# The first four units of a linear-attention kernel with a bilinear FFN: other places for loads, transfers and engine work

## The chip, the cores and the metric

The kernel runs on one core of one Trainium2 chip. The metric is the device time of one execution in microseconds (us), as a median of several runs. Before the change it is 614.28 us (three runs, 614.20 to 614.68).

## The reference

For each of 4 batches and 8 heads of width 48 a state of 48x48 is carried over 768 tokens; its result goes through a bilinear FFN.

```python
f = 1.0 / (1.0 + np.exp(-f_logit))
for t in range(S):                       # B, H, S, D = 4, 8, 768, 48
    state = f[:, :, t, :, None] * state + np.einsum('bhd,bhe->bhde', k[:, :, t], v[:, :, t])
    y[:, :, t] = np.einsum('bhd,bhde->bhe', q[:, :, t], state)
x = y.transpose(0, 2, 1, 3).reshape(B * S, H * D)         # 3072 x 384
out = (x @ w_a) * (x @ w_b) @ w_out                        # 384 -> 1536 -> 384
```

The inputs q, k, v and f_logit are float32. The three weights arrive as 64-bit floats, and the kernel makes float32 of them on the chip.

## The kernel before

**Units and blocks.** A unit is four heads of one batch over 384 tokens (BLK). Two units with the same tokens give the 384 columns of x for one block, so units 0 and 1 belong to block 0, units 2 and 3 to block 1, and there are 16 units and 8 blocks. What the change touches is the stretch in which units 0 to 3 run while the weights are still arriving; from unit 4 on a planner (`by_quotients`, from L1072) lays the work of the units beside the FFN's matmuls, with costs and due times that are written in the code.

**One unit** has these steps, each a function with one engine or two:
- `load_unit` (L196) issues its DMAs on the queue of SyncE (SP): two each for f, k and q, one for v. Three sets of buffers are used in turn, so unit 3 uses the set of unit 0.
- `front_parts` (L291) has four parts. Part 0 is two sigmoids on ScalarE (ACT) and a multiply-add on GpSimd (POOL). Parts 1 and 2 are running products on VectorE (DVE, L311 and L324). Part 3 multiplies k and q by them (L328). `next(fronts[u])` issues the next part.
- On TensorE (PE): `scores` (L382), `turn` (L406, a transposition of k), `within` (L480), `gains` (L430) and `across` (L501). Between them `mask` (L395, DVE), `turned` (L413 and L415, ACT) and `carried`/`carry` (L458 and L460, DVE, six small additions that carry the state from chunk to chunk). `hand_on` (L469) scales the last state for the next 384 tokens.
- `out_of_bank` (L520) copies y out of PSUM in three parts, on ACT or DVE. `stored` issues the transfers of y into xT (`store`, L542): five DMAs from SBUF to SBUF for each unit, since 48 rows of a head don't fall on whole blocks of 128.

**The FFN's first product.** `up(blk, ft)` (matmuls at L586) makes 128 of the 1536 columns of x @ w_b and x @ w_a for one block: 3 slices of x for b, then 3 for a, and each float32 matmul shows as two records, so 12 records for one `up`. It needs all of the block's xT. `product` copies b out of PSUM (ACT, L606) and multiplies (DVE, L608). Four PSUM banks serve two `up`s.

**The weights.** `weight_pieces` cuts them into 14 pieces of w_b and w_a, in turns (pieces 0 and 1 hold the columns of ft 0, 2 and 3 those of ft 1 and 2, 4 and 5 of ft 3 and 4, 6 and 7 of ft 5 and 6, and so on), and 6 of w_out. `load_weights` (L249, SP) loads the next piece into one of four places, or for pieces 4 and 5 into `groups`. `from_double` converts a piece: ACT L58 and L59 and POOL L60, then ACT L62 and L63, then DVE L68 and L70, which writes the float32 weights. `begin(n)` issues the steps of ACT and POOL up to piece n (begin(7.5) only the first half of the eighth), `end(n)` the DVE step up to n pieces; `end` also loads a further piece when it has ended one from the third on.

**What sets the order.** Each engine works in the order in which the code from L949 to L1069 issues the steps: the change touches this order, written out by hand. The queue of SP is in order too. The DMAs use eight semaphores in turn, so that a DMA is issued only when the one eight places ahead of it has landed. The buffers `at`, `kT` and `y` exist once; PSUM tiles ps_x and ps_y hold scores, transposed k, gains and y of a unit: for unit 2 its y is in ps_x, which unit 3's `turn` writes.

After the first five `up`s of block 0 a loop over `ups` converts a piece and runs an `up` in each turn, alternating blocks.

Of the kernel before, what the change touches and what calls it, by code (L numbers as in the profile page):

```python
# [48 lines left out]
        yield to, rows.rearrange("(k p) c -> p k c", p=128), (2, DM)  # L49


def from_double(nc, dst, raw, k, h, bit, sgn, whole):

    words = raw.bitcast(U32).rearrange("p k (n two) -> p (k n) two", two=2)
    lo, hi = words[:, :, 0], words[:, :, 1]
    width = lo.shape[1]
    h, bit, sgn = (x[:, 0:width] for x in (h, bit, sgn))
    nc.scalar.activation(h, hi.bitcast(FP32), AF.Abs, scale=HI_SCALE)  # L58
    nc.scalar.activation(bit.bitcast(FP32), lo, AF.Identity, bias=whole, scale=2.0**-29)  # L59
    nc.gpsimd.tensor_scalar(h, h, HI_MAX, None, ALU.min)  # L60
    yield
    nc.scalar.activation(sgn, hi.bitcast(FP32), AF.Sign)  # L62
    nc.scalar.activation(  # L63
        bit.bitcast(U16).rearrange("p (n two) -> p n two", two=2)[:, :, 1], sgn, AF.Relu, scale=-32768.0
    )
    yield
    hu = h.bitcast(U32)
    nc.vector.tensor_scalar(hu, hu, 3, None, ALU.logical_shift_left)  # L68
    hu, bit = (x.rearrange("p (k n) -> p k n", k=k) for x in (hu, bit))
    nc.vector.tensor_tensor(dst.bitcast(U32), hu, bit, ALU.add)  # L70
    yield


# [60 lines left out]
def by_quotients(ctx, tc, q, k, f_logit, v, moe_w_a, moe_w_b, moe_w_out, out, ident, weights, bad):  # L134
    nc = tc.nc
# [60 lines left out]
    def load_unit(u, names="fkqv"):  # L196
        for do in loads_of(u, names):
            do()
# [37 lines left out]
    def load_weights(n=1):  # L236
        for _ in range(n):
            if len(raws) == len(todo):
                return
            dst, src, (k, m) = todo[len(raws)]  # L240
            raw = dst
            if src.dtype != FP32:

                if len(raws) in EARLY:
                    raw = groups[:, EARLY.index(len(raws))].bitcast(mybir.dt.uint64)
                else:
                    raw = next(raw_places)
                raw = raw[:, 0:k * m].rearrange("p (k m) -> p k m", k=k)
            nc.sync.dma_start(out=raw, in_=src)  # L249
            raws.append(raw)  # L250

    def begin(n):

        while 2 * n > begun[0] < 2 * len(todo):
            i, second = divmod(begun[0], 2)
            dst, src, shape = todo[i]
            if not second:
                going.append(
                    from_double(nc, dst, raws[i], shape[0], next(blocks), bits[i % len(bits)], sign, whole)
                    if src.dtype != FP32 else iter(())  # L260
                )
            next(going[i], None)
            begun[0] += 1
# [153 lines left out]
    def gains(u, chunks=range(NC)):  # L417

        _, half, _ = unit(u)
        t, kT = sets[u % NSET], live[u]["kT"]  # L420
        last = half == NH - 1
        ps = live[u]["turned"]
        for n in range(2):
            for c in chunks:
                for p in range(2):
                    if last and c == NC - 1 and p == 1:
                        continue
                    for h in range(2):
                        r = slice(SUB * p, SUB * p + SUB)
                        nc.tensor.matmul(  # L430
                            ps[p][R * h:R * h + D, (n * NC + c) * D:(n * NC + c) * D + D],
                            lhsT=kT[r, n, c, R * h:R * h + D],
                            rhs=t["v"][r, n, c, h * D:h * D + D],
                            start=True,
                            stop=True,
                        )
        if chunks[0]:
            return
        st = sb3.tile([128, NJ, 2, D], FP32, tag="st", name="st")
        before = live[u - NQ]["st"][NJ] if half else None  # L440
        live[u]["st"] = [before] + [st[:, j] for j in range(NJ - 1 if last else NJ)]

    def carried(u, js=range(NJ)):

        for j in js:
            if j + 1 < len(live[u]["st"]):
                carry(u, j)
        if js[-1] == NJ - 1:
            hand_on(u)
            give_back(live[u]["turned"])  # L450

    def carry(u, j):
# [9 lines left out]
    def hand_on(u):  # L462

        if unit(u)[1] == NH - 1:
            return
        before = live[u]["st"][-1]
        for n in range(2):
            end = products_of_f[u][:, n, BLK - 1:BLK]
            nc.vector.tensor_scalar(before[:, n], before[:, n], end, math.exp(-MIDDLE), ALU.mult, ALU.mult)  # L469
# [40 lines left out]
    def out_of_bank(u, part):  # L510

        if not part:
            if u == NQ - 1:

                live[u]["y_sb"] = groups[:, 2 * NTG - 1, PIECE:].rearrange("r (o p m) -> r o p m", p=2, m=SUB)
            else:
                live[u]["y_sb"] = sb1.tile([128, 2 * NC, 2, SUB], FP32, tag="y", name="y")
        p, e, r, rows = ((0, 0, 0, 128), (1, R, 0, D), (1, 0, R, D))[part]
        copy = nc.vector.tensor_copy if u in FIRST and p else nc.scalar.copy
        copy(live[u]["y_sb"][r:r + rows, :, p], live[u]["y"][p][e:e + rows, 0:BLK].rearrange("r (o m) -> r o m", m=SUB))  # L520

    def stored(u):
# [6 lines left out]
    def stores_of(u):  # L529

        b, half, qd = unit(u)
        blk = b * NH + half

        def begin():
            if qd == 0:
                xT[blk] = sb2.tile([128, NKT, BLK], FP32, tag="xT", name="xT")
            live.pop(u - NQ, None)

        def store(n, h, kt, p, row, w):
            y = live[u]["y_sb"].rearrange("r (n c) p m -> r n (c p m)", n=2)  # L540
            queue = nc.scalar if u == NQ - 1 and n else nc.sync
            queue.dma_start(out=xT[blk][p:p + w, kt], in_=y[row:row + w, n])  # L542

        yield begin
        for n in range(2):
            for h in range(2):
                ch, row, left = (4 * qd + 2 * n + h) * D, R * h, D
                while left:
                    kt, p = divmod(ch, 128)
                    w = min(left, 128 - p)  # L550
                    yield partial(store, n, h, kt, p, row, w)
                    ch, row, left = ch + w, row + w, left - w
# [21 lines left out]
    def up(blk, ft):  # L574

        for _, _, _, do, *args in up_steps(blk, ft):
            do(*args)
# [353 lines left out]
    with tc.manual_schedule():  # L931
# [11 lines left out]
        def y_of(u):  # L943
            for part in range(3):
                out_of_bank(u, part)
            stored(u)
# [7 lines left out]
        for u in FIRST:  # L954
# [2 lines left out]
            load_weights()  # L957
            load_unit(u, "v")
        load_unit(2, "f")
        load_weights()  # L960
        for _ in range(3):
            next(fronts[0])
# [14 lines left out]
        carried(0, range(4))  # L977
        within(0)
        gains(1, range(NC - 1))
        mask(1)  # L980

        carried(1, range(1))
        carried(0, range(4, NJ))
        within(1)
        gains(1, range(NC - 1, NC))
        across(0)
        load_weights()
        carried(1, range(1, NJ))
        y_of(0)
        begin(3)  # L990
        across(1)
        y_of(1)
        end(2)


        load_unit(2, "k")
        load_unit(2, "q")
        load_weights()
        load_unit(2, "v")
        load_unit(3, "f")  # L1000
        load_weights()
        load_unit(3, "k")
        load_unit(3, "q")
        load_unit(3, "v")
        up(0, 0)
        begin(4)
        next(fronts[2])
        end(3)
        next(fronts[2])
        product()  # L1010
        end(4)
        next(fronts[2])
        load_unit(4, "f")
        up(0, 1)
        next(fronts[3])
        turn(2)
        turned(2)
        scores(2)
        mask(2)
        product()  # L1020
        begin(5)
        next(fronts[3])
        up(0, 2)
        within(2)
        gains(2)
        carried(2)
        begin(6)
        product()
        across(2)
        end(5)  # L1030
        y_of(2)
        load_weights()
        end(6)
        next(fronts[3])
        next(fronts[3])
        up(0, 3)
        product()
        begin(7)
        turn(3)
        turned(3)  # L1040
        scores(3)
        mask(3)
        up(0, 4)
        within(3)
        gains(3)
        carried(3)
        product()
        end(7)
        across(3)
        y_of(3)  # L1050
        load_unit(4, "k")
        load_unit(4, "q")
        load_unit(4, "v")
        load_weights()
        begin(8)
        end(8)


        ups = [(1, 0)]
        for i in range(5, NFT):  # L1060
            ups += [(1, i - 4), (0, i)]
        ups += [(1, i) for i in range(NFT - 4, NFT)]
        alone = len(todo) - 6
        for n, (blk, i) in enumerate(ups[0:alone]):
            convert(needed(i))
# [527 lines left out]
```

## Time and profile before

| | |
|---|---|
| median of three runs | 614.28 us |
| the profiled execution | 615.86 us |
| its span, first to last instruction | 614.1 us |
| busy: PE, weight loads, DVE, ACT, POOL | 574.0, 512.5, 411.4, 268.0, 76.2 us |
| PE busy from 200 to 600 us | 398.3 of 400 us |
| DMA moved | 49.42 MB |
| transfer of y into xT, SP, issue to landing | 2.2 us in the median |
| one `up` at the full clock (150 records in 48.54 us) | 3.9 us |

In the lines of the profile a row of ten or forty slices shows tenths of a slice. PEld is TensorE's weight load, which lies beside the matmuls. "A <- B" in a list of waits says that A waited until B was done, with the sum in us, how often, and the longest. SPq and ACTq are queues that issue DMAs. A group's "x5" is the number of its instructions.

### The profile page before, as it was taken

The page shows a single profiled execution, that of the slowest core. Times are in us where ns is not written, and L with a number is a line of the kernel's source. Part 1 is how long each engine was busy: PE and PEld are TensorE (multiplying, and loading weights), DVE is VectorE, ACT ScalarE, POOL GpSimd, SP SyncE. Part 2 cuts the span into 40 slices and gives each one's busy share as a digit, 9 for nine tenths or more (in the row PEclk, how much of TensorE's full clock was granted, in tenths as well). Part 3 has the DMA queues.
Part 4 walks back from the last instruction along what each step waited for, and adds up shares of the span by engine and source line. Part 5 has one row for each costly group of instructions (what it writes and reads, how often), then busy time and mean ns, then how long its engine had stood idle before and what let it go on. Part 6 is the DMA issues. An engine that isn't in the chain of part 4 may idle for free.

```text
span 614.1 us, 13863 instructions
## 1 busy us (share of the span) xinstructions
PE 574.0 (93%) x5778; PEld 512.5 (83%) x5778; DVE 411.4 (67%) x760; ACT 268.0 (44%) x505; POOL 76.2 (12%) x69
## 2 busy tenths in 40 slices
PE   1586889999999999999999999999999999999995
PEld 1444545555899999899989999999999999999995
DVE  6876424559997778885997569765866255836741
ACT  6627478984212345416541354316441244235300
POOL 6323144545300000000000000000000000000000
PEclk9878979999999999999999999999999999999998
DMA  8486698309955134016001440014001100000000
GB/s 216 142 231 175 181 226 260 128 1 166 187 129 139 36 96 96 3 35 166 23 3 33 114 101 2 2 35 109 1 3 46 36 11 1 1 27 0 1 28 31
DMA packets 33336, 49.42 MB, mean 80 GB/s; under 512 B 3952, under 2 KB 25072, under 8 KB 33264
## 3 DMA queue, kind: packets, MB, share of 16 engines
q1 hardware_dynamic: 30144, 42.53, 25.6%
q0 software_dynamic: 2992, 5.77, 5.6%
q8 instruction: 47, 0.77, 0.5%
q14 instruction: 25, 0.20, 0.1%
q10 hardware_dynamic: 128, 0.15, 0.1%
HBM read 33.23 MB, written 4.72 MB: 62 GB/s over the span
## 4 chain that ended last, share of the span: by engine, by line
PE 82%; DVE 8%; issue 3%; DMA 3%; ACT 2%; POOL 1%; SPq 1%; DVEq 0%; ACTq 0%; POOLq 0%
PE ps_f L708 34%; PE ps_f L801 26%; PE ps_f L586 13%; PE ps_y L501 2%; PE ps_y L480 2%; DVE sums L700 1%; PE ps_x L430 1%; DVE inv L324 1%; PE ps_x L382 1%; PE ps_x L406 1%; DMA groups<-in_moe_w_b_dram 1%; DVE groups L700 1%; POOL sums L60 1%; DMA q_in<-in_q_dram 1%; DVE groups L311 1%
## 5 line engine op out<-in xcount | busy, mean ns | idle before, releaser
L586 PE MATMUL ps_f<-xT,w_ba 128*128 128x384 f32 x288 | 105.1, 525 | 12.6 <-DMA xT<-y 7.4
L586 PEld LDWEIGHTS ps_f<-xT,w_ba 128*128 128x128 f32 x288 | 58.0, 205 | 55.6 <-issue 12.2
L1241 ACT COPY sums<-ps_f 128x384 f32<-128x384 f32 x120 | 57.3, 480 | 76.1 <-PE ps_f L708 59.9
L1241 ACT COPY groups<-ps_f 128x384 f32<-128x384 f32 x120 | 57.7, 481 | 62.9 <-PE ps_f L708 39.9
L708 PE MATMUL ps_f<-xT,w_ba 128*128 128x192 f32 x384 | 78.4, 327 | 0.0
L708 PEld LDWEIGHTS ps_f<-xT,w_ba 128*128 128x128 f32 x384 | 64.8, 190 | 0.2
L708 PE MATMUL ps_f<-groups,w_ba 128*128 128x192 f32 x288 | 55.4, 327 | 0.0
L708 PE MATMUL ps_f<-x_sums,raw 128*128 128x192 f32 x288 | 54.0, 331 | 1.2 <-DVE groups L700 0.9
L801 PE MATMUL ps_f<-w_out,sums 128*128 128x192 f32 x288 | 52.2, 329 | 0.0
L801 PE MATMUL ps_f<-w_out,groups 128*128 128x192 f32 x288 | 51.7, 328 | 0.0
L708 PEld LDWEIGHTS ps_f<-x_sums,raw 128*128 128x128 f32 x288 | 46.9, 190 | 4.3 <-DVE groups L700 1.8
L801 PE MATMUL ps_f<-spare,sums 128*128 128x192 f32 x288 | 49.0, 326 | 0.0
L708 PEld LDWEIGHTS ps_f<-groups,w_ba 128*128 128x128 f32 x288 | 47.9, 190 | 0.5 <-ACT groups L1241 0.3
L60 POOL TENSOR_SCALAR sums<-sums 128x768 f32<-128x768 f32 (+1 forms) x20 | 40.9, 2046 | 58.5 <-ACT sums L58 58.4
L801 PEld LDWEIGHTS ps_f<-w_out,sums 128*128 128x128 f32 x288 | 47.1, 190 | 0.9 <-DVE o L836 0.5
L801 PEld LDWEIGHTS ps_f<-w_out,groups 128*128 128x128 f32 x288 | 47.1, 190 | 0.7
L801 PEld LDWEIGHTS ps_f<-spare,sums 128*128 128x128 f32 x288 | 47.1, 190 | 0.1
L307 POOL TENSOR_SCALAR inv<-inv 128x768 f32<-128x768 f32 x14 | 13.0, 925 | 266.1 <-ACT inv L304 266.0
L700 DVE TENSOR_TENSOR sums<-sums,groups 128x768 f32<-128x768 f32 x36 | 34.7, 965 | 14.2 <-ACT groups L1241 13.7
L700 DVE TENSOR_TENSOR sums<-ps_f,sums 128x384 f32<-128x384 f32 x60 | 32.9, 553 | 16.5 <-PE ps_f L708 15.0
L708 PE MATMUL ps_f<-x_sums,w_ba 128*128 128x192 f32 x192 | 39.3, 327 | 0.5 <-DVE sums L700 0.5
L708 PE MATMUL ps_f<-xT,raw 128*128 128x192 f32 x192 | 39.4, 328 | 0.0
(134 smaller groups left out, 852.2 us busy)
## 6 DMA issues: line engine op xcount, KB each, us to landing
raw<-w_ba POOLq DMA_DIRECT2D x11, 512.0 KB, 8.3
k_in<-in_k_dram SPq DMA_DIRECT2D x32, 144.0 KB, 3.4
q_in<-in_q_dram SPq DMA_DIRECT2D x32, 144.0 KB, 4.1
v_in<-in_v_dram SPq DMA_DIRECT2D x16, 288.0 KB, 5.2
raw<-in_moe_w_out_dram SPq DMA_DIRECT2D x6, 768.0 KB, 4.3
out_dram<-o SPq DMA_DIRECT2D x24, 192.0 KB, 2.0
f_in<-in_f_logit_dram SPq DMA_DIRECT2D x28, 144.0 KB, 3.0
xT<-y SPq DMA_DIRECT2D x45, 72.0 KB, 2.2
```

Source lines behind the costliest of these rows:

```text
L60: nc.gpsimd.tensor_scalar(h, h, HI_MAX, None, ALU.min)
L307: nc.gpsimd.tensor_scalar(inv, inv, EXP_K, 1.0, ALU.mult, ALU.add)
L311: nc.vector.tensor_tensor_scan(F[:, c], F[:, c], none, math.exp(MIDDLE), ALU.mult, ALU.add)
L324: nc.vector.tensor_tensor_scan(inv[:, w], inv[:, w], none[:, 0:C], first, ALU.mult, ALU.add)
L382: nc.tensor.matmul(ps[h][SUB * p:SUB * p + SUB, o:o + SUB], lhsT=kf[r, tokens(n, c, p)], rhs=qf[r, tokens(n, c, p)], start=True, stop=True,)
L480: nc.tensor.matmul(ps[p][e:e + D, o:o + SUB], lhsT=t["v"][r, n, c, h * D:h * D + D], rhs=at[r, h, o:o + SUB], start=o == 0, stop=True, ski ...
L501: nc.tensor.matmul(ps[p][e:e + D, o:o + SUB], lhsT=st[j][r, n], rhs=qf[r, tokens(n, c, p)], start=False, stop=True, skip_group_check=True,)
L586: nc.tensor.matmul(ps[nm][:, 0:BLK], lhsT=w[:, kt, ft * 128:ft * 128 + 128], rhs=xT[blk][:, kt], start=kt == 0, stop=kt == NKT - 1,)
L700: nc.vector.tensor_tensor(to, x, y, op)
L708: nc.tensor.matmul(ps[:, g], lhsT=sums_of_w[name][:, g, 128 * j:128 * j + 128], rhs=sums_of_x[blk][name], start=start and g == 0, stop=Tru ...
L801: nc.tensor.matmul(to, lhsT=x[:, i // 2, i % 2], rhs=w[:, NI * (i % 2) + i // 2], start=start and i == 0, stop=i == HFT - 1, skip_group_ch ...
L1241: do(*args)
```

## The change

Five things change, all in the stretch of the first four units, and one in the conversion.

1. **Loads.** Pieces 2 and 3, k, q and v of unit 2, f of unit 3 and piece 4 are issued on SP right behind f of unit 2, ahead of the transfers of y of units 0 and 1. Before they stood behind these. Pieces 5 and on stay behind.
2. **y of units 0 and 1.** Both units' copies out of PSUM come ahead of both units' transfers. Of unit 1 two of three copies are on ACT (before one). Unit 0's first two transfers and unit 1's last two go over ACT's queue (before only unit 1's last two).
3. **State.** The last of the six additions and `hand_on` of units 0 and 1 go behind the transfers. `end(1)` (DVE's step of piece 0) goes ahead of unit 1's `mask`, `end(2)` behind the transfers.
4. **Orders of the engines for units 2 and 3.** Among others: all of unit 2's front directly behind `up(0, 0)`, `turn` and `scores` of unit 2 ahead of `up(0, 1)`, `within` and `gains` of unit 2 ahead of `up(0, 2)`, `turn` and `scores` of unit 3 ahead of `up(0, 3)`, and `end(8)` ahead of unit 3's transfers (before behind them).
5. **The loop's order.** `up(0, 5)` comes first, ahead of `up(1, 0)`.
6. **Conversion.** L70 for pieces of w_b and w_a becomes three instructions, one for each slice of 128 rows, where it was one.

```diff
-def from_double(nc, dst, raw, k, h, bit, sgn, whole):
+def from_double(nc, dst, raw, k, h, bit, sgn, whole, apart=False):
...
-    nc.vector.tensor_tensor(dst.bitcast(U32), hu, bit, ALU.add)
+    dst = dst.bitcast(U32)
+
+    for rows in ([slice(i, i + 1) for i in range(k)] if apart else [slice(0, k)]):
+        nc.vector.tensor_tensor(dst[:, rows], hu[:, rows], bit[:, rows], ALU.add)
...
-                    from_double(nc, dst, raws[i], shape[0], next(blocks), bits[i % len(bits)], sign, whole)
+                    from_double(
+                        nc, dst, raws[i], shape[0], next(blocks), bits[i % len(bits)], sign, whole, shape[0] == NKT
+                    )
...
         if js[-1] == NJ - 1:
-            hand_on(u)
             give_back(live[u]["turned"])
...
-        copy = nc.vector.tensor_copy if u in FIRST and p else nc.scalar.copy
+        copy = nc.vector.tensor_copy if u in FIRST and part > u else nc.scalar.copy
...
-            queue = nc.scalar if u == NQ - 1 and n else nc.sync
+            queue = nc.scalar if u in FIRST and n == u else nc.sync
...
         load_unit(2, "f")
+        load_weights(2)
+        load_unit(2, "k")
+        load_unit(2, "q")
+        load_unit(2, "v")
+        load_unit(3, "f")
         load_weights()
...
         gains(1, range(NC - 1))
+        end(1)
         mask(1)
 
         carried(1, range(1))
-        carried(0, range(4, NJ))
+        carried(0, range(4, 5))
         within(1)
         gains(1, range(NC - 1, NC))
         across(0)
-        load_weights()
-        carried(1, range(1, NJ))
-        y_of(0)
-        begin(3)
-        across(1)
-        y_of(1)
-        end(2)
-
-
-        load_unit(2, "k")
-        load_unit(2, "q")
-        load_weights()
-        load_unit(2, "v")
-        load_unit(3, "f")
-        load_weights()
+        carried(1, range(1, 5))
+        for u in FIRST:
+            if u:
+                across(u)
+            for part in range(3):
+                out_of_bank(u, part)
+        for u in FIRST:
+            stored(u)
+        begin(3)
+        end(2)
+        for u in FIRST:
+            carried(u, range(5, NJ))
+            hand_on(u)
+
+
         load_unit(3, "k")
         load_unit(3, "q")
         load_unit(3, "v")
+        load_weights()
         up(0, 0)
+        for _ in range(3):
+            next(fronts[2])
         begin(4)
-        next(fronts[2])
-        end(3)
-        next(fronts[2])
-        product()
+        next(fronts[3])
         end(4)
-        next(fronts[2])
+        turn(2)
+        scores(2)
         load_unit(4, "f")
         up(0, 1)
-        next(fronts[3])
-        turn(2)
-        turned(2)
-        scores(2)
         mask(2)
         product()
+        turned(2)
         begin(5)
         next(fronts[3])
-        up(0, 2)
+        next(fronts[3])
         within(2)
         gains(2)
+        product()
         carried(2)
         begin(6)
-        product()
+        next(fronts[3])
+        up(0, 2)
         across(2)
-        end(5)
+        end(6)
         y_of(2)
         load_weights()
-        end(6)
-        next(fronts[3])
-        next(fronts[3])
-        up(0, 3)
-        product()
-        begin(7)
         turn(3)
         turned(3)
         scores(3)
+        begin(7)
+        product()
+        up(0, 3)
         mask(3)
-        up(0, 4)
+        begin(7.5)
         within(3)
         gains(3)
+        product()
         carried(3)
-        product()
-        end(7)
+        begin(8)
+        up(0, 4)
+        end(8)
         across(3)
         y_of(3)
         load_unit(4, "k")
         load_unit(4, "q")
         load_unit(4, "v")
         load_weights()
-        begin(8)
-        end(8)
-
-
-        ups = [(1, 0)]
-        for i in range(5, NFT):
-            ups += [(1, i - 4), (0, i)]
-        ups += [(1, i) for i in range(NFT - 4, NFT)]
+        product()
+
+
+        ups = [(0, 5), (1, 0)]
+        for i in range(6, NFT):
+            ups += [(1, i - 5), (0, i)]
+        ups += [(1, i) for i in range(NFT - 5, NFT)]
```

## The prediction

> **What bounds the kernel now.** I read the slices of the span first, to find where TensorE (PE) isn't full.
>
> ```profile
> PE   1586889999999999999999999999999999999995
> ACT  6627478984212345416541354316441244235300
> PEclk9878979999999999999999999999999999999998
> DMA  8486698309955134016001440014001100000000
> ```
>
> A slice is 15.35 us. From the sixth on (80 us) PE is full to the end, so that a us is won only ahead of 80 us, and what is won there arrives at the end as long as the later work waits for PE alone. Next, that stretch by windows: PE, weight loads, DVE, ACT, POOL busy, then granted clock, DMA share.
>
> ```profile
> 27.00:31.30 4.30, 0.29 (x18) 0.14 (x6) 3.92 (x9) 2.08 (x4) 0.00 (x0) 0.80 0.30 76
> 31.30:44.40 13.10, 12.07 (x24) 6.16 (x25) 10.89 (x18) 3.41 (x5) 3.32 (x2) 0.67 0.89 239
> 44.40:54.00 9.60, 8.27 (x203) 5.75 (x201) 5.24 (x10) 8.45 (x12) 4.43 (x3) 1.00 1.02 265
> 54.00:58.10 4.10, 0.01 (x1) 0.04 (x1) 2.14 (x4) 3.19 (x6) 1.01 (x1) 0.85 0.12 38
> 58.10:74.40 16.30, 15.01 (x215) 9.52 (x215) 9.03 (x20) 5.18 (x7) 2.12 (x1) 0.83 0.64 188
> 74.40:80.20 5.80, 2.43 (x4) 0.71 (x5) 1.97 (x3) 5.03 (x7) 2.12 (x1) 0.76 0.24 61
> 80.20:84.20 4.00, 3.99 (x7) 2.18 (x8) 0.51 (x1) 2.33 (x4) 0.98 (x1) 0.50 1.06 223
> ```
>
> PE has three holes (27 to 31.3, 54 to 58.1, 74.4 to 80.2), and behind each a stretch at half the clock, where it looks busy and does half the work. The waits from 31 to 81 us say why:
>
> ```profile
> ACT spare L304 <- DMA f_in<-in_f_logit_dram: 8.4, 1, 8.4
> PE ps_f L586 <- DMA xT<-y: 7.4, 3, 4.0
> PE ps_f L586 <- DVE w_ba L70: 4.4, 2, 4.2
> DVE groups L608 <- ACT x_sums L606: 4.3, 2, 3.0
> DVE w_ba L70 <- PE ps_f L586: 1.3, 1, 1.3
> ```
>
> ACT stands 8.4 us (37.1 to 45.5) until unit 3's f has landed, and all conversions behind it in ACT's order come late. So piece 4 is ready (L70) only at 57.9, and `up(0, 3)` waits 4.2 us. The waits for xT are the first and the third hole. The transfers and loads on SP's queue, in order of time:
>
> ```profile
> 27.71 3.20 SPq L542 DMA_DIRECT2D xT<-y  x5
> 31.01 1.81 SPq L542 DMA_DIRECT2D xT<-groups  x3
> 32.91 1.01 SPq L208 DMA_DIRECT2D k_in<-in_k_dram  x2
> 34.92 0.42 SPq L249 DMA_DIRECT2D groups<-in_moe_w_b_dram  x1
> 35.97 0.89 SPq L208 DMA_DIRECT2D f_in<-in_f_logit_dram  x2
> ```
>
> Eight transfers of y take SP 5 us to issue; the last lands at 34.13. Unit 2's and 3's loads stand behind them, though the DMA engines were idle from 23.3 (landing of piece 3) to 27.7.
>
> **What the Trainium skill says.** "TensorE: Matmul & The Clock Gate", Part 1: after an idle window of some 3.4 us PE runs at half its clock, and returns after a busy window; windows run freely. The trace agrees: the granted clock is 0.5 from 29.60 to 39.84, 56.91 to 63.73 and 77.39 to 84.21, all multiples of 3.41. "DMA: Bandwidth & Descriptors", Queues, rings and completion order: SP and ACT own one ring each on the same DMA engines, a ring is worked off in order, and the engines alternate between rings. The trace agrees: piece 5, behind other loads, lands 12.0 us after its issue, a transfer of y with nothing ahead 2.2 us. "SBUF — State Buffer", Who interferes with whom: a DVE operation with two SBUF inputs and a reading POOL operation exclude each other. L60 took 2.65 us beside DVE's scan and 2.12 alone; I add up to 0.5 us per meeting.
>
> **The change, part by part.**
>
> *Loads ahead.* k, q, v of unit 2, f of 3 and piece 4 are 1920 KB. From the landing of unit 2's k (35.76) to piece 7 (56.62) 4944 KB came, 237 KB per us, so they end 8.1 us after piece 3 (23.33): 31.4. f of unit 3 lands near 28 (before 45.4): ACT's 8.4 us go. The price is that SP's transfers of y, issued from 27, stand in the ring behind piece 4 and land after 31.4.
>
> *y over two queues.* Ahead of unit 1's additions DVE has three instructions less (one of 0.27 us, two of 0.25 to 0.8), and ahead of the copies three more of them, so across(1) starts 0.2 to 0.8 us sooner than 26.42, and all copies are done near 27.7 (before 29.6). SP issues six transfers at 0.6 us from 27.1, ACT four at 0.64 from 27.7. The eighth waits for the one eight places ahead, piece 4. The last lands at about 31.4 + 2 = 33.3 (31.5 to 36): 0.8 us sooner than before, not the 2 us that the issue times alone would give. ACT is held some 3 us by issuing; it isn't late for that, since its next work is needed at 38.
>
> *Rows of L70.* One operation is 0.96 us (1536 elements) or 0.56 (768), so 0.16 + 0.52 ns per element; three of 512 cost 1.1 us where they follow on each other. That is 0.2 us more per piece; at least 0, at most 0.5. It stays beside PE. What goes is DVE's wait for PE (1.3 us here, 9.9 us over all pieces): a slice's columns no longer span those that PE reads.
>
> *PE's line*, with one `up` 3.9 us (150 records in 48.54 us) and 7.7 at half clock (12 x 0.64); turn 0.65, scores 0.75, within 0.8, gains 0.65, across 0.7 from the chain:
> - `up(0, 0)`: first slices from 31.7, all from 33.3, at half clock: to 39.4. Meanwhile DVE does end(2) 1.1, the state 1.5, unit 2's front 6.3, pieces 2 and 3 3.3 (to 40.5), none late.
> - turn, scores to 41; `up(0, 1)` to 44.9; within, gains to 46.4 (mask 42; ACT's turned 41); `up(0, 2)` 50.3; across 51.0. Before, the same work was done at 53.9.
> - turn(3) writes ps_x, from which ACT copies unit 2's y: three copies, 1.46: hole to 52.6. scores to 54.0. Piece 4 is ready at 53.5, piece 5 at 55: ACT has both done by 49, at 3.6 us a piece.
> - `up(0, 3)` to 57.9 (before 65). mask(3) stands on DVE behind product of `up(0, 2)`, whose copy stands on ACT behind turned(3) and piece 6: 52.6 + 0.8 + 0.8 + 3.6 + 0.5 = 58.3, product 58.8, mask 59.75: hole of 1.85.
> - within, gains 61.2; `up(0, 4)` 65.1; across(3) 65.8. Unit 3's xT takes 5.65 us from there as before (74.42 to 80.07), so to 71.5; loads of pieces 9 and 10 ahead of it end at about 69.5 (unit 5's loads start at 55.2, and the same row took 9.1 us from first landing to piece 9, then 2.5 for 10) and cost nothing more.
> - `up(0, 5)` lies under that, to 69.7; two slices of `up(1, 0)` to 71; it goes on at 71.5.
>
> Before, `up(1, 0)` went on at 80.2 without `up(0, 5)`. The lead is 80.2 - (71.5 - 3.9) = 12.6. To it comes the half clock from 80.2 to 84.2 that had cost 2.0. The two new holes (1.6 and 1.85) may drop the clock; a window of 3.4 at half costs 1.7, and at somewhat over even odds I take 1.0. **Sum: 13.6 us.** Cover gone: without `up(0, 5)` under the transfers, 3.9 us come back.
>
> *After it.* The loop has ACT busy 4.0 of 3.92 us per turn, yet it needs piece 9 at its sixth turn, and the pieces stand ready some 6 us early (L70 of piece 9 at 97.6, needed at 104), so nothing new is late. The planner's part starts behind the loop in every engine's own order and moves as a whole; ±1 us.
>
> The profiled execution was 615.86 around a span of 614.1, the median 614.28. So 614.1 - 13.6 = 600.5 of span, 602.3 profiled, and **600.7** as a median.
>
> **The rivals.**
> 1. *y late behind the bulk loads.* If piece 4 lands at 33 and the transfers behind the eighth wait for it too, the last lands at 36.2, 2.9 late; one more cold window 1.7, and ACT held at its queue 1.5 more: 606.8. For it: SP's ring is in order, and the eight semaphores. Against: ACT's ring passes it by.
> 2. *The clock in the holes.* Both holes trip it, for one or two windows each: 3.4 to 6.8 instead of 1.0, so 603 to 606.5; I take 604.5. From 73.97 to 77.39 PE was busy 1.3 us and fell; from 70.56 to 73.97 it was busy over 2 and did not.
> 3. *More is won.* The holes close (ACT ahead of my times), the clock returns a window sooner (1.7): 13.6 + 1.6 + 1.85 + 1.0 = 18: 596.3.
> 4. *Given back later.* The conversions in the loop become the bound, since ACT there is full: 614.3, no change. Against it: those 6 us in hand.
> 5. *Slower.* PE never gets a busy window between the holes and stays at half clock to 71: PE's 6 x 3.9 + 2 x 3.6 = 30.7 us become 61, less the some 4 lost anyway: 27 us against 13.6 won, 627. It decides from 27 us of added half clock. Against it: three `up`s stand nearly unbroken from 41 to 51.
>
> That the change doesn't do what it says is hardly open: the order is the code's.
>
> **Numbers.** Forecast 55% (597.5 to 603.5), rival 1 17%, rival 2 10%, rival 3 10%, rival 4 5%, rival 5 3%. The range 595.5 to 607 leaves out rivals 4 and 5, some of 1 and the tail of 3. What differs by under 0.2% (1.2 us) can't be told from no change: same 3% (of rival 4), slower 4% (5 and the rest of 4), faster 93%.
>
> **What would show it.** f of unit 3 landing near 28, and ACT's wait for it gone; no wait of DVE L70 for PE; the last y near 33; a hole of 1.6 us at turn(3) (ACT y) and one near 58 (DVE at); `up(1, 0)` going on near 71.5; half clock only up to 40. I am wrong if the last y lands after 36, if half clock returns from 50 to 70, or if PE has holes beyond 75 us that it hadn't.

## The result, and the profile after

The changed kernel takes **605.27 us** (median of four runs, 603.99 to 605.66), against 614.48 us (four runs) of the kernel before beside it: a ratio of 0.9844 [0.9826, 0.9862]. The profiled execution has 605.66 us and a span of 603.9, before 615.86 and 614.1. The forecast was 600.7 for the median and 600.5 for the span: of 13.6 us, 10.2 came in the span and 9.2 in the medians. A second measure is used below, the time at which PE begins its eighth `up`: from about there PE is full, and the number holds only what the first units cost. It is 88.72 us before and 78.26 after, 10.5 us less.

The slices of the span of the changed kernel, 15.1 us each:

```profile
PE   1668899999999999999999999999999999999995
ACT  6567779963132455326521354326331335134300
PEclk9969999999999999999999999999999999999999
DMA  8963897059854233044003420032001100000000
```

PE is full from the sixth slice on (before from the seventh); a low clock is left in the third alone, where four of the first six had shown it. The same windows as in the prediction (PE, weight loads, DVE, ACT, POOL busy, granted clock, DMA share, GB/s):

```profile
27.00:31.30 4.30, 1.06 (x40) 0.77 (x40) 2.51 (x7) 0.95 (x2) 0.00 (x0) 1.00 0.80 249
31.30:44.40 13.10, 9.37 (x67) 5.28 (x68) 11.40 (x27) 8.49 (x12) 3.99 (x3) 0.61 0.63 192
54.00:58.10 4.10, 2.49 (x101) 2.11 (x92) 3.25 (x9) 2.38 (x5) 0.00 (x0) 1.00 0.14 39
74.40:80.20 5.80, 5.36 (x17) 3.07 (x18) 0.44 (x1) 5.26 (x7) 3.02 (x2) 1.00 0.96 197
80.20:84.20 4.00, 4.00 (x14) 2.41 (x13) 3.45 (x10) 3.77 (x5) 2.32 (x1) 1.00 1.11 217
```

The second hole (54 to 58.1) has shrunk to 1.6 us, of the third (74.4 to 80.2) 0.5 us is left, and the half clock behind it is gone. The first has moved and grown: it lies from 28.7 to 34.1, with half clock behind it to 42.1, so that it reaches into the second window (9.37 of 13.10 us, clock 0.61). The waits from 31 to 81 us:

```profile
PE ps_f L590 <- DMA xT<-y: 5.8, 2, 5.3
ACT y L524 <- PE ps_y L505: 3.9, 1, 3.9
PE ps_x L411 <- ACT y L524: 1.6, 1, 1.6
PE ps_y L484 <- DVE at L400: 1.3, 1, 1.3
```

ACT's 8.4 us for unit 3's f and DVE's and PE's waits at the last step of a piece (L70, now L73) are no longer in the list; PE's longest wait for xT went from 4.0 to 5.3. SP's queue shows why. First its own waits between 20 and 40 us, then what it issued (start, duration):

```profile
SPq L211 <- DMA raw<-in_moe_w_a_dram: 6.3, 1, 6.3
SPq L546 <- DMA xT<-y: 4.5, 1, 4.5
```
```profile
25.17 1.91 SPq L211 DMA_DIRECT2D f_in<-in_f_logit_dram  x2
27.12 0.43 SPq L252 DMA_DIRECT2D groups<-in_moe_w_b_dram  x1
32.13 1.87 SPq L546 DMA_DIRECT2D xT<-y  x3
34.10 1.80 SPq L546 DMA_DIRECT2D xT<-groups  x3
```

and ACT's queue in the same stretch:

```profile
28.80 0.60 ACTq L546 DMA_DIRECT2D xT<-y  x1
```

A transfer of y waits for a transfer of y: SP's first one goes out only at 32.13, after ACT's first (issued 28.80) has landed at 32.06. Both use the same one of the eight semaphores (number 101 in the trace), which are handed round over both queues together. So SP stood 4.5 us, and for 4.0 of them unit 0's y was ready (its last copy ends at 28.09).

Pieces 2 and 3, which "The change" counts among the loads put ahead, stood ahead of y before too (issued at 12.80 and 13.42 in that trace). What moved ahead is k, q and v of unit 2, f of unit 3 and piece 4, 1920 KB.

### The profile page after: what moved, and what is told of

It reads as the page before. It is cut to its first block, busy times and chain, and to the rows that moved or that the text cites. A ratio compares the mean times of both kernels' runs of the same rounds, so it can differ in the third digit from the quotient of the medians.

```text
span 603.9 us, 13889 instructions
## 1 busy us (share of the span) xinstructions
PE 568.9 (94%) x5778; PEld 510.5 (85%) x5778; DVE 414.0 (69%) x787; ACT 268.8 (45%) x506; POOL 75.3 (12%) x69
## 3 DMA queue, kind: packets, MB, share of 16 engines
HBM read 33.23 MB, written 4.72 MB: 63 GB/s over the span
## 4 chain that ended last, share of the span: by engine, by line
PE 84%; DVE 9%; issue 2%; ACT 2%; DMA 1%; SPq 0%; DVEq 0%; ACTq 0%
PE ps_f L712 35%; PE ps_f L805 27%; PE ps_f L590 14%; PE ps_y L484 2%; PE ps_y L505 2%; PE ps_x L387 2%; DVE sums L704 1%; DVE inv L329 1%; PE ps_x L435 1%; PE ps_x L411 1%; DVE groups L704 1%; DVE f_in L316 1%; DVE q_in L333 1%; DVE at L400 1%; DVE groups L316 1%
## 5 line engine op out<-in xcount | busy, mean ns | idle before, releaser
L590 PE MATMUL ps_f<-xT,w_ba 128*128 128x384 f32 x288 | 99.2, 503 | 6.8 <-DMA xT<-y 5.8
L590 PEld LDWEIGHTS ps_f<-xT,w_ba 128*128 128x128 f32 x288 | 55.2, 195 | 45.9 <-DMA xT<-y 6.6
L712 PEld LDWEIGHTS ps_f<-xT,w_ba 128*128 128x128 f32 x384 | 64.8, 190 | 0.2
L712 PE MATMUL ps_f<-xT,raw 128*128 128x192 f32 x192 | 39.4, 328 | 0.0
```

The lines of the kernel that those rows point to most:

```text
L590: nc.tensor.matmul(ps[nm][:, 0:BLK], lhsT=w[:, kt, ft * 128:ft * 128 + 128], rhs=xT[blk][:, kt], start=kt == 0, stop=kt == NKT - 1,)
L712: nc.tensor.matmul(ps[:, g], lhsT=sums_of_w[name][:, g, 128 * j:128 * j + 128], rhs=sums_of_x[blk][name], start=start and g == 0, stop=Tru ...
```

## The experiments

Each kernel is the changed one with one edit, unless said otherwise. They ran in three groups, each on a chip of its own: runs 1 to 4, 5 to 8 and 9 to 12. The kernel before had medians of 613.33, 614.16 and 614.15 us in them, so that between groups the ratio is the safer number. **Theory 1**: the gain is short of the forecast because y of units 0 and 1 lands late, held by the loads that were put ahead and by semaphores in turn over two queues; all else shifts with it. **Rivals**: the clock; other waits that take the place of y's; or another part of the change (conversion in rows, the loop's order) carries or loses the time.

| kernel | median, us | ratio to before | last y lands | eighth `up` |
|---|---|---|---|---|
| before | 614.15 | 1 | 34.13 | 88.72 |
| changed | 605.27 | 0.9844 [0.9826, 0.9862] | 37.21 | 78.26 |
| changed, again | 605.56 | 0.9851 [0.9833, 0.9868] | 37.99 | 79.42 |
| y on one queue | 604.96 | 0.9871 [0.9853, 0.9889] | 35.39 | 76.40 |
| piece 4 behind y | 603.54 | 0.9845 [0.9831, 0.9858] | 35.31 | 75.67 |
| loop as before | 611.48 | 0.9963 [0.9950, 0.9977] | 38.09 | 85.17 |
| one instruction for L73 | 605.76 | 0.9877 [0.9862, 0.9892] | 37.90 | 78.37 |
| all loads behind y | 606.41 | 0.9873 [0.9853, 0.9893] | 32.66 | 78.22 |
| PE kept warm | 604.77 | 0.9835 [0.9815, 0.9855] | 37.34 | 77.69 |
| four edits at once | 603.76 | 0.9830 [0.9811, 0.9850] | 36.84 | 75.51 |
| only f of unit 3 ahead | 602.49 | 0.9808 [0.9787, 0.9830] | 33.03 | 74.83 |
| the same, product early | 602.58 | 0.9820 [0.9797, 0.9843] | 32.55 | 75.19 |
| only f ahead, y on one queue | 604.80 | 0.9851 [0.9826, 0.9876] | 35.87 | 76.96 |
| before, with the loads ahead | 616.31 | 1.0033 [1.0021, 1.0045] | 37.83 | 88.91 |

The last two columns come from one profiled execution of each kernel (before's, of 615.86 us, is a long one). The changed kernel, run again as it is, differs by 0.8 us at the last y and by 1.2 at the eighth `up`, and the four medians of before lie up to 1.2 apart (613.33 to 614.48). Differences of 1.2 us and less are read as nothing here.

**1. y on one queue.**

```diff
-            queue = nc.scalar if u in FIRST and n == u else nc.sync
+            queue = nc.sync
```

> The changed kernel, with all ten transfers of y of units 0 and 1 on SP's queue. Theory 1 (shared semaphores: in the changed kernel SP's first transfer stood 4.5 us until ACT's first had landed, since it takes its semaphore in turn): without ACT's transfers SP's first is issued at about 28.2 instead of 32.1, ten follow at 0.6, the last lands near 35.8 instead of 37.2, and the time falls by about 1.4 us. Rival (two queues save issue time): four more transfers at 0.6 on one queue come on top, the last lands 2.4 us later, and the time rises by about 2.4 us.

SP's first transfer of y goes out at 27.52 instead of 32.13, since ACT takes no semaphore any more, and the tenth, issued at 33.23, lands at 35.39: 1.8 us before that of two queues. The eighth `up` is 1.9 us sooner. The time shows nothing of it: the median is 0.3 below, and the ratio to its own group's before (0.9871) above the changed kernel's 0.9844. So with these loads ahead the second queue makes y later where it was meant to make it sooner; that this costs time isn't shown. Nor is the semaphore all that this edit changes: piece 4 goes out at 24.32 instead of 27.12 and lands at 30.35 instead of 31.82. The waits of SP in this kernel have none of y for y:

```profile
SPq L252 <- DMA raw<-in_moe_w_a_dram: 4.5, 1, 4.5
SPq L546 <- DVE y L524: 3.3, 1, 3.3
```

**2. Piece 4 behind y.**

```diff
         load_unit(3, "f")
-        load_weights()
...
         for u in FIRST:
             stored(u)
+        load_weights()
         begin(3)
```

> The changed kernel, with the load of piece 4 behind the transfers of y; k, q, v of unit 2 and f of unit 3 stay ahead. Theory 1 (shared semaphores): ACT's first transfer lands at 31.0 instead of 32.1, SP's second waits for it, the last lands near 35.4, and the time falls by about 1.7 us. Rival (it is the bytes of piece 4 in the ring that hold y up): y goes as in the prediction's sum, the last lands near 33.3, and the time falls by 3.9 us.

ACT's first transfer, without 768 KB in front of it, lands at 30.75 and after 2.14 us instead of 3.27. SP's first is free here (27.63), its second waits for ACT's first and goes at 30.77; the last y lands at 35.31 and the eighth `up` starts 2.6 us sooner. The median is 2.2 us below that of run 4, of the same group, which starts its eighth `up` as the changed kernel does; the ratio (0.9845) is the changed kernel's own (0.9844), so that a gain in time isn't clear. SP's wait for y is down from 4.5 to 2.5 us and not to nothing: the load is one part of the delay and the semaphore another.

```profile
SPq L546 <- DMA xT<-y: 2.5, 1, 2.5
```

**3. The loop's order as before** (`ups` begins with (1, 0), and `up(0, 5)` stands at its old place).

> The changed kernel, with the loop in the order of before, up(1, 0) ahead of up(0, 5). Theory (up(0, 5) is the cover of unit 3's transfers): a hole of some 4 us near 70 to 75, the time rises by 3.9 us, and by up to 2 more if the clock halves behind the hole. Rival (the transfers aren't what ends last there, the conversions of pieces 6 and 7 are): no change within 1 us.

PE has a hole of 4.56 us for unit 3's xT, and the clock is at half from 73.40 to 80.23; the eighth `up` is 6.9 us later and the median 6.2 us (5.7 beside run 4 of the same group).

```profile
75.79 10.51 PE L590 MATMUL ps_f<-xT,w_ba 128*128 128x384 f32 x25 [4.56 <-DMA xT<-y]
```

So the one line of the order of `ups` is worth more than half of the whole gain: an `up` under the transfer (3.9 us) and the clock that it keeps up.

**4. L73 in one instruction** (`apart` never set).

> The changed kernel, with DVE's last step of a piece in one instruction again. Theory (it lies beside PE): DVE waits for PE again, some 0.3 us each in the first 70 us and up to 3 us each in the loop, and the time stays within 0.4 us. Rival (it is a sizeable part of the gain): the waits reach PE through late pieces, and the time rises by over 1.3 us.

The eighth `up` is at 78.37 against 78.26, the span 604.0 against 603.9, the median 0.5 above: no difference. The three rows take away a wait of DVE (9.0 us over all pieces here), which PE didn't feel: it has no wait for L73. The ratio lies 0.0033 above the changed kernel's, 2 us, mostly since before was faster in this group; the changed kernel didn't run in it, so that a small worth of the rows isn't ruled out.

**5. The changed kernel once more**, as a control for the scatter.

> The changed kernel as it is, beside the other kernels of this group and the kernel before, for a common base. Both theories: a ratio of 0.984 to the kernel before, and a lead of some 10 us where the eighth up begins.

605.56 us. One thing is longer in its profile, a stop of PE within across(1), which the last section takes up.

**6. All loads behind y**: k, q and v of unit 2, f of unit 3 and piece 4 as in the kernel before, all else as changed.

```diff
-        load_unit(2, "k")
-        load_unit(2, "q")
-        load_unit(2, "v")
-        load_unit(3, "f")
-        load_weights()
...
             stored(u)
+        load_unit(2, "k")
+        load_unit(2, "q")
+        load_weights()
+        load_unit(2, "v")
+        load_unit(3, "f")
         begin(3)
```

> The changed kernel, with k, q, v of unit 2, f of unit 3 and piece 4 behind the transfers of y, as before the change. Theory 1 (the loads ahead end ACT's wait for f of unit 3, and cost some of it by making y late): y's last lands near 34 instead of 37.2, but unit 2's k and q land near 38 and unit 3's f near 44, ACT stands up to 6 us for it, and the time rises by 3 to 6 us. Rival (with the new order of the engines the loads needn't be ahead): y's earlier landing decides, and the time falls by 2 to 3 us.

Theory 1's size for this run missed. The last y lands at 32.66, with both queues unhindered, and `up(0, 1)` starts 4.6 us sooner (39.71). But by the eighth `up` nothing is left of it (78.22), and the median is 606.41:

```profile
ACT spare L309 <- DMA f_in<-in_f_logit_dram: 8.3, 1, 8.3
PE ps_y L435 <- ACT kT L420: 2.4, 1, 2.4
```

ACT's wait for unit 3's f is back at its old length, and PE now waits 2.4 us for ACT at `gains` of unit 2, at half clock from 47.32 on; `up(0, 2)` starts 8.3 us after `up(0, 1)` instead of 5.4. So here the loads ahead save at ACT about what they cost at y. That suggested a split: of the loads, ACT needs only f, 288 of 1920 KB.

**7. PE kept warm** (eight added matmuls of 128x384 ahead of `up(0, 0)`, whose result is not used).

```diff
         for u in FIRST:
             stored(u)
+        for _ in range(8):
+            nc.tensor.matmul(ps_x[:, 0, 0:BLK], lhsT=ident, rhs=halves(sets[0]["q"])[:, 0:BLK], start=True, stop=True)
```

> The changed kernel, with eight float32 matmuls of 128x384 added on PE between across of unit 1 and up(0, 0), where PE stands idle; their product is overwritten and nothing of the computation is left out. Theory (half the clock is a cost of the hole, not of the work): the clock stays at 1.0 past 31.9, up(0, 0) ends 2.7 us sooner, and the time falls by 2 to 2.7 us, less what DVE, with pieces 2 and 3 ready only at 41.4 and 43.1, keeps back. Rival (DVE's pieces bind there, or the added matmuls make up(0, 0) late): no change within 0.6 us, or slower.

The clock stays full until 36.59 and is at half for one window (36.59 to 40.00), where the changed kernel is at half for three (31.85 to 42.09). `up(0, 1)` starts 1.0 us sooner, yet another window at half comes at 57.06, and the eighth `up` gains 0.6 us, which is nothing by the scatter. Of the changed kernel's 10.2 us at half, 4.8 lie ahead of 36.67, where PE mostly waits for y; of the 5.4 in `up(0, 0)` 3.2 are left here, since the one window falls there. At half, 5.4 us cost at most 2.7, and the forecast had counted half clock up to 39.4 there itself: little of its missing time can lie in the clock.

**8. Four edits at once**: piece 4 behind y, five of the matmuls of run 7, unit 1's y copied by ACT alone (`part > 2 * u` for `part > u`), and the product of `up(0, 2)` ahead of `end(6)`.

> The changed kernel with four edits: piece 4's load behind the transfers of y; five added matmuls in PE's hole ahead of up(0, 0); the product of up(0, 2) ahead of the DVE step of pieces 4 and 5, so that its copy no longer stands on ACT behind piece 6; all three copies of unit 1's y on ACT, so that DVE isn't held. If the four causes add: y's last lands near 35.3, up(0, 0) ends near 38, up(0, 1) near 43.6, across(2) starts near 49.2, the hole of 1.3 us at mask(3) is gone, up(1, 0) goes on near 69, and the time falls by some 6 us below the changed kernel. Rival (one binds after another, DVE's pieces first): 2 to 3 us.

603.76 us and 75.51, no better than run 2 alone (603.54 and 75.67). The hole at `mask(3)` is gone, but a stop of PE of 2.4 us in across(1) makes y late again. Four edits in one kernel tell little; the next runs go back to one.

**9. Only f of unit 3 ahead.**

```diff
-        load_unit(2, "k")
-        load_unit(2, "q")
-        load_unit(2, "v")
         load_unit(3, "f")
-        load_weights()
...
             stored(u)
+        load_unit(2, "k")
+        load_unit(2, "q")
+        load_weights()
+        load_unit(2, "v")
         begin(3)
```

> The changed kernel with only one of the loads ahead of y: unit 3's f, while unit 2's k, q, v and piece 4 go behind y, as in the kernel before. Theory 1 (y's transfers are late for the loads that SP must issue and for the semaphores that ACT's transfers take in turn with them; ACT's wait for f needs f alone ahead): SP's first y transfer goes out by 27.5 us, the last y lands at 33 to 34 us (37.2 changed, 32.7 with all loads behind), unit 3's f lands before 29 us and PE has no hole at gains(2) (2.4 us with all loads behind); the third up starts at 45.5 us, the eighth at 75 to 76 us (78.3 changed): 602 to 603 us, 2.5 to 3.5 us below the changed kernel. Rival (whatever the loads save or cost, the next wait takes it, as with all loads behind): the eighth up starts at 78 us, 605 us.

As theory 1 had it. SP's queue in this kernel:

```profile
27.16 2.43 SPq L546 DMA_DIRECT2D xT<-y  x3
29.69 1.81 SPq L546 DMA_DIRECT2D xT<-groups  x3
31.55 1.07 SPq L211 DMA_DIRECT2D k_in<-in_k_dram  x2
```

The first transfer goes out at 27.16, the last lands at 33.03, and ACT doesn't wait for f, nor PE for `gains`. The eighth `up` is at 74.83, 3.4 us sooner than changed; the span is 600.8 against 603.9, and the median 602.49 us. Unit 2's k and q land at 34.6 to 37.1, which is early enough. This is the best version found: 0.9808 [0.9787, 0.9830] of the time before.

**10. The same with the product of `up(0, 2)` ahead of `end(6)`.**

> As the run with unit 3's f alone ahead, and the product of up(0, 2) is put in front of the end of a load's conversion behind across(2), two places earlier on DVE. Theory 1: the hole at mask(3) and within(3), 1.3 us in the changed kernel, closes, and nothing else is late for it: the eighth up starts at 74 to 75 us, 601 to 602 us. Rival: the hole only moves to the piece whose conversion is then later, the eighth up starts where it does without this edit, and the time is the same within 0.7 us.

The rival was right in size, by another way: 602.58 us, eighth `up` at 75.19. With f alone ahead, PE's wait at `mask(3)` isn't in the profile to begin with: in run 9 PE is at half clock from 54.27 to 57.68, in `up(0, 3)`, so that DVE is there in time. Here `up(0, 3)` starts later, at 55.88 instead of 54.22, and `up(0, 4)` at 61.63 instead of 61.32.

**11. Only f ahead, and y on one queue** (edits 9 and 1).

> As the run with unit 3's f alone ahead, all ten y transfers on SP's queue. Theory 1: with no other load in front, the ten go out from 27 to 32.7 us at 0.55 to 0.65 us each and the last lands at 35 us, 1.5 to 2 us after that of two queues: here the second queue pays, while in the changed kernel with its loads ahead it cost 1.8 us. Eighth up at 77 us, 604 us. Rival (the second queue pays in neither): the last y within 0.5 us of the run with two.

The last y lands at 35.87, 2.8 us after that of two queues, the eighth `up` is 2.1 us later and the median 2.3. Beside run 1 this tells the second queue's worth for y: it brings the last landing 2.8 us forward where no load stands between, and puts it 1.8 us back where loads ahead bind the semaphores. In the time the first shows (2.3 us, one group), the second doesn't.

**12. The kernel before with only the loads ahead.**

> The kernel before with only the loads ahead: unit 2's k, q, v, unit 3's f and piece 4 are issued ahead of y's transfers, all else in the old order. Theory 1 (the loads ahead give back at y what they save at ACT; the order and the loop bring the gain): ACT's wait of 8.4 us for f is gone, the last y lands 2 to 5 us later than the 35.3 us of before, the hole of 4.2 us that waits for a piece's last step stays: the eighth up starts at 87 to 89 us (88.7 before), 612.5 to 614.5 us. Rival (the loads ahead alone carry most of the gain, since ACT's wait of 8.4 us was what held the first units): the eighth up at 82 us, 607 to 608 us.

616.31 us, 1.0033 [1.0021, 1.0045] of before, and the eighth `up` at 88.91 against 88.72: no gain, and the rival is out. The median is 2.2 us above before's, of which the eighth `up` shows 0.2; where the rest goes isn't known. (In before's trace the last y lands at 34.13, not at the 35.3 that the expectation names; here it lands at 37.83.) ACT's 8.4 us are gone, and where the time goes can be followed from `up` to `up`. `up(0, 1)` and `up(0, 2)` start 3.5 us later than before, for y. PE's hole for L70 ahead of `up(0, 3)` is 2.2 us instead of 4.2, so that this one starts 1.5 us later; half clock lasts one window behind it instead of two, and `up(0, 4)` starts 0.4 us later, the eighth 0.2. So the loads ahead do win back 3.3 of the 3.5 us that y lost, 2.0 of them at the hole for L70 and most of the rest with one window at half less, and nothing is left over. SP's wait for y is there too:

```profile
SPq L542 <- DMA xT<-groups: 3.4, 1, 3.4
```

With all loads behind y the other parts alone give 0.9873 (run 6), the loads alone 1.0033: the gain comes from the other parts. Of these run 3 shows the loop's order to be worth more than half, and run 4 finds nothing for the rows at the eighth `up`; no run takes apart the orders for units 2 and 3, y's copies and the state.

## Why the prediction was right, and where it was short

- **Loads ahead.** Right in effect (f of unit 3 at 28.1 and 29.3, forecast 28; piece 4 at 31.82, forecast 31.4; ACT's wait gone), wrong in what it was taken to cost. The price named was that SP's transfers of y "stand in the ring behind piece 4", and that is SP's ring only.
- **y over two queues: the term that failed.** "The last lands at about 31.4 + 2 = 33.3": it landed at 37.21, 3.9 us late, and so behind the 36 that the prediction had set as a sign of being wrong. Three things are in it.
  - ACT's first transfer was taken to go at 27.7 and went at 28.80. The copies were done at 30.3 and not 27.7. across(1) began at 26.97, where 0.2 to 0.8 us *sooner* than 26.42 was forecast (DVE's step of piece 0 now stands ahead of `mask(1)`, which begins at 23.25 instead of 22.90), and PE stopped within it for 0.68 us.
  - That transfer took 3.27 us to land and not 2.2. It landed 0.24 us behind piece 4, and in runs 3, 4 and 5 0.19 to 0.23 us behind it (0.80 in run 7); with piece 4 put behind y (runs 2 and 8) it took 2.1. The 3.27 us are not the loads' mark alone, though: in run 9 ACT's first took 3.00 us with no load of the kernel in flight.
  - The step let the eighth of the ten transfers wait for piece 4, as if all ten had been dealt their semaphores behind it. In the trace ACT's four have 101, 104, 106 and 107; between these stand SP's v of unit 2 (102) and the first half of f of unit 3 (105), and only behind them the second half (108) and piece 4 (109). So the one eight places ahead of SP's *first* transfer, 101 again, was ACT's first, and SP stood until 32.06.

  Run 9's 33.03 lies near the forecast 33.3, but that is chance: no piece 4 stands ahead there, and the issue times alone would by the prediction have given some 32.1 (2 us less than before's 34.13).
- **Rival 1** has the same place and nearly the same size (last y 36.2), and half of the mechanism: it let SP's transfers stand behind piece 4, and not SP's queue behind ACT's landing. The reason against it, "ACT's ring passes it by", didn't hold: ACT's first landed behind piece 4, as said. At 606.8 its time is 1.5 above the result, the forecast 4.6 below: the result lies within the stated range, but nearer to this rival.
- **PE's line after y.** Everything is shifted by 3 to 4 us and little else. `up(0, 1)` started at 44.26 (forecast 41.0), `up(0, 2)` at 49.67 (46.4), `up(0, 3)` at 57.90 (54.0), `up(0, 4)` at 64.68 (61.2), `up(0, 5)` at 69.57 (65.8). `up(1, 0)` went on at 74.84 (71.5). The hole at `turn(3)` is 1.6 us as forecast, that at `mask(3)` 1.3 and not 1.85.
- **The clock.** The 1.0 us put down for the new holes was not lost: half clock ends at 42.09 (forecast 40) and comes back only at the very end. Rival 2 is out for this kernel, but not by much: in six of the ten edited forms of it (run 9 among them) a window at half falls between 47 and 61 us.
- **Rows.** 1.10 us for three instructions, as worked out, beside PE, and worth nothing that the profile shows (run 4).
- **The loop's order.** "[W]ithout `up(0, 5)` under the transfers, 3.9 us come back": 6.9 at the eighth `up` (run 3), since the hole also brings two windows of half clock. The mechanism was right, the cover undervalued.
- **The sum.** 13.6 - 3.9 (y) + 1.0 (clock not lost) + 0.5 (`mask(3)`) = 11.2 against 10.2 in the span and 9.2 in the medians; 1 to 2 us aren't resolved. That two smaller terms came out better than forecast, and so made up for part of y, is luck.

What isn't settled: how much of y's delay is the loads' bytes and how much the semaphore. Run 1 takes away ACT's semaphores (but adds issue time and lets piece 4 go out sooner), run 2 part of both; each gave 1.8 to 1.9 us at the last y. And why each variant's end differs by 1 us and more from what its lead says isn't explained.

## What to carry to other kernels

A load moved ahead is paid for by what it is moved past: list what each queue still has to issue behind it and put ahead only what an engine waits for (here 288 of 1920 KB, 3 us faster than with all of it ahead). Before a second queue is used, look whether its DMAs share semaphores in turn with the first; here they did, and SP stood until ACT's transfer had landed. A removed wait is worth what reaches the bound engine's line, less what the removal delays: with the loads alone ahead (run 12) ACT's wait of 8.4 us was gone, PE won back 3.3 us, and y had cost as much, while one `up` put under a transfer was worth 7.

## What was not expected of the hardware

**PE stopped within across(1) for nothing that the profile shows.** The forty matmuls are issued without a break in some kernels and with one in others. In the changed kernel the last 32 of them begin 0.68 us after the first eight have ended:

```profile
27.98 0.76 PE L505 MATMUL ps_y<-q_in,st 48*48 48x64 f32 x32 [0.68 <-issue]
```

What goes with the stop is the time of a transfer on the DMA queue that the profile names "instruction". In these kernels one such transfer begins between 23.5 and 26.25 us (in steps of 0.25 us):

```
transfer begins, us       stop of PE in across(1), us
23.50 to 24.00            none   (before, all loads behind, only f ahead and its two variants)
24.75, 25.00              0.30, 0.41   (PE kept warm, piece 4 behind y)
25.25                     0.99, 1.01   (one instruction for L73, loop as before)
25.50                     0.68, 0.92, 1.55   (changed, y on one queue, changed again)
26.00                     2.34, 2.37   (before with loads ahead, four edits)
```

The later the transfer, the longer the stop, and the transfer is late where more than f was put ahead. No run moved that transfer alone: this is a correlation over 14 kernels, and the cause of the stop stays open.

**The windows of the clock begin at another time in every run.** Within a run the clock changes in steps of 3.41 us (31.85 to 42.09 is three of them), but where they lie differs: in the two runs of the same changed kernel half clock for `up(0, 0)` ended at 42.09 and at 43.63, and over the kernels without added matmuls anywhere from 36.1 to 43.6 us. A window at half costs up to 1.7 us (half of 3.41). Between those two runs it cost less: of the 1.2 us by which their eighth `up` differs, 0.8 are there at the last y, behind the longer stop of PE (1.55 against 0.68 us), and 0.4 are left for the clock.
